# Moving the preparation of the next chunk, and one leaky relu, behind the copies of the finished output banks, in a spectral layer followed by a two-layer MLP

## The chip, the cores and the metric

One core of one Trainium2 chip. The metric is the device time of one execution in microseconds (us), the median of several runs. The engines named here are PE (TensorE; PEld is its weight load), DVE (VectorE), ACT (ScalarE), POOL (GpSimd) and SP (SyncE, which here only issues DMAs). All matmuls of the main loop run on fp32 data that is split into a high and a low fp32r part.

## The reference

Input x is (8, 3008, 256). First a spectral layer, then an MLP with leaky relu on all 24064 tokens:

```
X  = rfft(x, axis=1)
Yr = Xr @ w_r - Xi @ w_i + b_r ;  Yi = Xr @ w_i + Xi @ w_r + b_i
Y  = sign(Y) * max(|Y| - 0.01, 0)            # for Yr and Yi each
y  = irfft(Y, n=3008, axis=1).reshape(24064, 256)
h  = y @ w_in                                # 256 x 2048
out = max(0.01 * h, h) @ w_out               # 2048 x 256
```

## The kernel before

The length 3008 is 47 x 64, so the transform is done in two stages of small matmuls: `fwd` (the stage over 47), then `mid` (the stage over 64, the projection by w_r and w_i, the threshold, and the first inverse stage). They pass through DRAM as `u_dram` and `v_dram`. The second inverse stage, `inverse`, reads `v_dram` through the tile `vin` (one buffer, loaded by `v_load` on the SP queue) and writes tokens into the tiles `yc` (three buffers).

The MLP works on 32 chunks of 752 tokens, four to a batch; a chunk is two halves of 376. `moe()` is the main loop, and each chunk has two parts.

The **product part** loops over the eight q (256 of the 2048 hidden columns each). `moe_a` and `moe_b` compute the 2 x 2 block product by seven block products instead of eight, so the inputs are needed in seven combinations, the "forms" in the tile `yhl` (one buffer, high and low part). Each product is three matmuls of 376 columns into a bank `psh`. `moe_a` needs the forms 0, 3, 4 and 2 in this order, `moe_b` the forms 1, 6 and 5. ACT and DVE then add and apply the leaky relu (ACT `Prelu`). The first half's result `gf` is split at once into `gh` (ACT, L625) and `gl` (DVE, L626). The second half's result `gs` gets its leaky relu at L615 and waits in `s_t`; `late` splits it in the output part. Between `moe_a` and `moe_b` run the output products of the first half, two q behind.

The **output part** has 16 steps, each one call of `moe_o` (six matmuls into one of the two banks `pso`). The first four steps finish the two banks of the first half; ACT copies each to `ob` (L650) and SP stores it. The next steps need those two banks again, for the second half. `late` runs on the way: it splits `gs` of the next q into one of three pairs of `gg` buffers, as PE frees them. Also on the way, `forms(ci + 1)` prepares the next chunk: five pieces, each a few DVE subtractions and splits (L525 on ACT, L526 on DVE).

`fwd`, `mid` and the next chunk's `inverse` calls are streams that are mixed in between: the tokens generator takes one step per half q (16 per product part), `fwd` and `mid` advance with the position in the loop, such that the stream of a batch ends before the position `read[b]` at which `v_load` wants it.

What sets the order: the program is given in the order of these generators, and a planner issues each engine's instructions by that order as priority and by when its own timeline says that they are ready. `issue_after(x)` puts instructions behind x on x's engine; `in_order` keeps the MLP's matmuls in program order on PE. An instruction of a stream may be moved far ahead of its place. On the chip every engine then runs its list in order.

Of the kernel before, what the change touches and what calls it, by code (L numbers as in the profile page):

```python
# [12 lines left out]
AF = mybir.ActivationFunctionType  # L13
# [10 lines left out]
SLOPE = 0.01  # L24
# [6 lines left out]
def spectral_mlp_kernel(  # L31
# [17 lines left out]
    NB = x.shape[0]  # L49
# [5 lines left out]
    NQ = NF // 2  # L55
    HT, HP = N1 * N2 // 8, 192
    CT, HH = 2 * HT, HT // 2
# [8 lines left out]
    sync, act, dve, pool = nc.sync, nc.scalar, nc.vector, nc.gpsimd  # L66

    def bank(tag, bufs):
        return ps.tile([P, 512], F32, name=tag, tag=tag, bufs=bufs)
# [30 lines left out]
    def turned_halves(t):  # L100
        return t[:, :, :HH].rearrange("p a b -> p b a")

    def halves(t):
        return t.rearrange("p (a b) -> p a b", a=2)
# [47 lines left out]
        dve.tensor_mul(q, q, wl.bitcast(F32))  # L152


    made, converted, parted, early_parts = [], [], [], []


    NIN = DF // 4
# [310 lines left out]
    nch = p0[-1] // CT  # L469
    y_t, v_t, f_t, h_t, g_t, o_t, s_t = {}, {}, {}, {}, {}, {}, {}  # L470

    def v_load(pi):
        if pi == 1:
            vin = early[:PA, :4 * D].rearrange("p (c i d) -> p c i d", c=2, i=2)
        else:
            vin = sb.tile([PA, 2, 2, D], F32, name="vin", tag="vin", bufs=1)
        (b, s, _), n = pairs[pi][0], len(pairs[pi])
        vv = v_dram[b].rearrange("c k (g s) d -> c (k g) s d", g=NG)
        for c in range(2):
            ld = sync.dma_start(vin[:, c, :n, :], vv[c, :, s:s + n, :])  # L480
            if pi < 2:
                reads.append(ld)
        v_t[pi] = vin

    def inverse(pi, eh):


        n0, m = pairs[pi][0][2], sum(n for _, _, n in pairs[pi])
        ne, n = m * NK1, m * N1
        vin = v_t[pi]  # L490
        py = bank("psf", 2)
        s = slice(eh * P, (eh + 1) * P)
        for c in range(2):
            for i in range(len(pairs[pi])):
                o = c * ne + i * n0 * NK1
                nc.tensor.matmul(py[:, o:o + P], vin[:, c, i, s], consts["ga"][:, c, :], start=True, stop=True)  # L496
        odd = sb.tile([P, 2 * NG * NK1], F32, name="odd", tag="odd", bufs=1)[:, :ne]
        y = sb.tile([P, 2 * NG * N1], F32, name="y", tag="y")
        act.copy(odd, py[:, ne:2 * ne])
        dve.tensor_add(y[:, :ne], py[:, :ne], odd)  # L500
        ev, ov = (t.rearrange("p (m k) -> p m k", k=NK1)[:, :, 1:] for t in (py[:, :ne], odd))
        dve.tensor_sub(y[:, ne:n].rearrange("p (m k) -> p m k", m=m), ev, ov)
        lo = p0[pi]
        while lo < p0[pi + 1]:
            k = lo // HT
            hi = min((k + 1) * HT, p0[pi + 1])
            if k not in f_t:
                f_t[k] = sb.tile([P, NH, HT], F32, name="yc", tag="yc", bufs=3)
            act.copy(f_t[k][:, eh, lo - k * HT:hi - k * HT], y[:, lo - p0[pi]:hi - p0[pi]])
            lo = hi  # L510
# [49 lines left out]
    def product(dst, ci, q, k, start=False):  # L560
        form(dst, ci, q, AK[k - 1], BK[k - 1], start)

    def plain(ci, q, half):

        g0 = sb.tile([P, 2, 2, HP], F32, name="gs" if half else "gf", tag="gs" if half else "gf", bufs=NQ if half else 1)
        g = g0[:, :, :, :HH]
        for i, ((a, b), (a1, b1)) in enumerate((((0, 0), (1, 1)), ((3, 0), (2, 4)))):
            c = bank("psh", 4)
            form(c, ci, q, a, 2 * half + b, True)
            form(c, ci, q, a1, b1 + half if i else 2 * half + b1)  # L570
            act.activation(g[:, i], halves(c[:, :HT]), AF.Prelu, alpha=SLOPE)
        if half:
            s_t[ci, q] = g0
        else:
            parts(ci, q, 0, g0)
            early_parts[:] = parted
# [19 lines left out]
    def moe_b(ci, q):  # L596

        if ci == 0:
            return plain(ci, q, 1)
        c11, c21, c12, u, g1 = h_t.pop((ci, q))  # L600
        product(c11, ci, q, 2)
        product(c21, ci, q, 4)
        product(c12, ci, q, 3)
        g0 = sb.tile([P, 2, 2, HP], F32, name="gf", tag="gf", bufs=1)
        g = g0[:, :, :, :HH]
        act.activation(g[:, 0], halves(c11[:, :HT]), AF.Prelu, alpha=SLOPE)  # L606
        dve.tensor_add(g[:, 1], halves(c21[:, :HT]), halves(u))  # L607
        act.activation(g[:, 1], g[:, 1], AF.Prelu, alpha=SLOPE)  # L608
        g = g1[:, :, :, :HH]
        dve.tensor_add(g[:, 0], halves(c12[:, :HT]), halves(u))  # L610
        parts(ci, q, 0, g0)
        early_parts[:] = parted
        g = wide(g)
        with tc.issue_after(parted[0].ins):
            act.activation(g, g, AF.Prelu, alpha=SLOPE)  # L615
        s_t[ci, q] = g1

    def wide(t):
        return t.rearrange("p i a b -> p (i a) b")

    def parts(ci, q, half, g):
        gh, gl = g_t[ci, q, half] = tuple(
            sb.tile([P, 2, 2, HP], F32R, name=n_, tag="gg", bufs=6) for n_ in ("gh", "gl"))
        g, h, l = (wide(t)[:, :, :HH] for t in (g, gh, gl))
        cp = act.copy(h, g)  # L625
        parted[:] = [cp, dve.tensor_sub(l, g, h.bitcast(F32))]  # L626
# [5 lines left out]
    def moe_o(ci, q, h, eh):  # L632
        gh, gl = g_t[ci, q, h]
        wh, wl = consts["wout"]
        if q == 0:
            o_t[ci, h, eh] = bank("pso", 2)
        po = o_t[ci, h, eh][:, :HT]
        pv = po.rearrange("p (b a) -> p b a", a=2)
        s = slice(eh * P, (eh + 1) * P)
        for j, (a, r) in enumerate(((wh, gh), (wl, gh), (wh, gl))):  # L640
            for i in range(2):
                f = 2 * q + i
                mlp[:] = [nc.tensor.matmul(  # L643
                    pv, a[:, f, s], turned_halves(r[:, i]), start=(f == 0 and j == 0),
                    stop=(f == NF - 1 and j == 2),
                )]
        if q == NQ - 1:
            ob = sb.tile([P, HT], F32, name="ob", tag="y")
            with tc.high_priority(200):
                act.copy(ob, po)  # L650
            lo = ci * CT + h * HT
            sync.dma_start(out[s, lo:lo + HT], ob)

    due = [[p for p in range(len(pairs)) if p0[p] // CT == ci] for ci in range(nch)]
    UNITS = 45 * NQ
    read = [max(0, b * nch // NB - 1) + 51 / UNITS for b in range(NB)]

    def tokens(ci):

        for _ in range(3):  # L660
            yield
        for p in due[ci]:
            v_load(p)
            yield
            yield
            for eh in range(NH):
                inverse(p, eh)
                yield
                yield

    def moe():

        behind = []

        def next_o(eh, least=2):
            if len(behind) >= least:
                in_order(moe_o, *behind[0], eh)
                if eh:
                    behind.pop(0)

        for ci in range(nch):
            nxt = tokens(ci + 1) if ci + 1 < nch else iter(())
            units = 0
            for q in range(NQ):
                in_order(moe_a, ci, q)
                next_o(0)
                next(nxt, None)
                units += 18
                yield ci + units / UNITS
                in_order(moe_b, ci, q)  # L690
                next_o(1)
                behind.append((ci, q, 0))
                next(nxt, None)
                units += 15
                yield ci + units / UNITS
            for _ in nxt:
                pass
            nxt = forms(ci + 1) if ci + 1 < nch else iter(())
            behind += [(ci, q, 1) for q in range(NQ)]
            late(ci, 0)  # L700
            for q in range(0, NQ, 2):
                for k, eh in ((0, 0), (1, 0), (0, 1), (1, 1)) if q < 4 else ((0, 0), (0, 1), (1, 0), (1, 1)):
                    in_order(moe_o, *behind[q + k], eh)
                    if eh:
                        late(ci, q + k + 1)
                    with tc.issue_after(early_parts[0].ins), tc.issue_after(early_parts[1].ins):
                        next(nxt, None)
                    units += 6
                    yield ci + units / UNITS
            del behind[:NQ]  # L710
        while behind:
            for eh in range(NH):
                next_o(eh, 1)
# [215 lines left out]
```

## Time and profile before

| what | value |
|---|---|
| median of 3 runs | 2504.17 us (2503.83 to 2505.91) |
| the profiled execution | 2500.98 us |
| its span from first to last instruction | 2499.2 us |
| PE busy | 2419.7 us (97%) |
| DVE busy | 1848.5 us (74%) |
| ACT busy | 1652.7 us (66%) |
| POOL busy | 251.3 us (10%) |

The busy time of PE is a union of overlapping matmuls whose ends are modelled; what tells of lost time is when a matmul starts later than the one before it allows. The granted TensorE clock is full (1.00) from 130 us on. From chunk 8 on, at 746 us, the pattern of four chunks repeats batch after batch; the last batch has no more stream beside it from chunk 27 on.

### The profile page before, as it was taken

To read this page: it belongs to the slowest core of one execution; us is meant where nothing else is said; L and a number is where in the kernel's file an instruction comes from. 1 tells how busy PE (TensorE), PEld (TensorE's weight loads), DVE (VectorE), ACT (ScalarE), POOL (GpSimd) and SP (SyncE) were. 2 spreads that over 40 slices of the span, in tenths; PEclk is the share of its full clock that TensorE was granted. 3 is DMA by queue.
4 is the path that set the end of the run, shared out by engine and by line. 5 is a ranking of instruction groups with operands and counts; after the bars stand their busy time and mean duration, and the time that the engine had idled before them with its cause. 6 is when DMAs were issued, how large, how long until landed. Compare 5 with 4: busy or idle time off the path is not lost.

```text
span 2499.2 us, 41562 instructions
## 1 busy us (share of the span) xinstructions
PE 2419.7 (97%) x15412; PEld 2326.9 (93%) x15412; DVE 1848.5 (74%) x3197; ACT 1652.7 (66%) x3229; POOL 251.3 (10%) x192
## 2 busy tenths in 40 slices
PE   6899999999999999999999999999999999999999
PEld 4589999999999999999999999999999999999999
DVE  6777778777787777776787777777778777777675
ACT  4676766677667666676766676666766667756555
POOL 1200113000110001100021000210012000000000
PEclk8999999999999999999999999999999999999999
DMA  7632214221232112321132121331214211110000
GB/s 236 184 116 57 59 45 128 70 56 53 71 101 59 51 51 79 95 62 51 47 93 85 53 61 45 96 87 45 61 40 119 68 51 46 42 37 29 17 13 19
DMA packets 138479, 173.68 MB, mean 69 GB/s; under 512 B 15661, under 2 KB 100645, under 8 KB 138277
## 3 DMA queue, kind: packets, MB, share of 16 engines
q1 hardware_dynamic: 97688, 124.17, 16.7%
q10 hardware_dynamic: 40589, 46.87, 7.5%
q8 instruction: 121, 1.98, 0.3%
q14 instruction: 81, 0.66, 0.1%
HBM read 95.22 MB, written 75.76 MB: 68 GB/s over the span
## 4 chain that ended last, share of the span: by engine, by line
PE 79%; ACT 9%; DVE 5%; DMA 3%; issue 2%; SPq 0%; ACTq 0%; POOL 0%; DVEq 0%
PE pso L643 33%; PE psh L98 29%; PE psf L82 11%; PE psf L496 3%; PE psf L365 2%; ACT gh L625 1%; ACT zf L417 1%; DMA vin<-v_dram 1%; DVE t L407 1%; ACT gs L615 1%; ACT zf L413 1%; PE psh L82 1%; DMA v_dram<-v 1%; ACT gf L608 1%; DVE gf L607 1%
## 5 line engine op out<-in xcount | busy, mean ns | idle before, releaser
L98 PE MATMUL psh<-yhl,win_hi 128*128 128x376 f32 x3600 | 894.8, 331 | 16.1 <-DVE gs L592 14.3
L98 PEld LDWEIGHTS psh<-yhl,win_hi 128*128 128x128 f32 x3600 | 607.4, 190 | 45.6 <-DVE gs L592 22.8
L98 PE MATMUL psh<-yhl,win_lo 128*128 128x376 f32 x1800 | 580.5, 322 | 0.0
L643 PE MATMUL pso<-gh,wout_hi 128*128 128x376 f32 x2048 | 496.6, 324 | 9.4 <-ACT ob L650 9.2
L643 PE MATMUL pso<-gl,wout_hi 128*128 128x376 f32 x2048 | 497.7, 325 | 0.8 <-DVE gl L626 0.6
L643 PE MATMUL pso<-gh,wout_lo 128*128 128x376 f32 x2048 | 493.3, 322 | 0.0
L643 PEld LDWEIGHTS pso<-gh,wout_hi 128*128 128x128 f32 x2048 | 354.3, 189 | 13.0 <-ACT ob L650 12.3
L643 PEld LDWEIGHTS pso<-gl,wout_hi 128*128 128x128 f32 x2048 | 354.1, 189 | 7.8 <-DVE gl L626 6.4
L643 PEld LDWEIGHTS pso<-gh,wout_lo 128*128 128x128 f32 x2048 | 356.6, 189 | 0.0
L98 PEld LDWEIGHTS psh<-yhl,win_lo 128*128 128x128 f32 x1800 | 340.0, 189 | 0.3 <-issue 0.2
L626 DVE TENSOR_TENSOR gl<-gf,gh 128x752 fp32r<-128x752 f32 x256 | 244.6, 956 | 115.9 <-ACT gh L625 114.5
L399 POOL TENSOR_TENSOR kb<-bias,kc 128x512 f32<-128x512 f32 x96 | 138.9, 1447 | 1592.3 <-ACT kc L397 1516.0
L626 DVE TENSOR_TENSOR gl<-gs,gh 128x752 fp32r<-128x752 f32 x256 | 238.8, 939 | 53.6 <-ACT gh L625 52.5
L606 ACT ACTIVATE gf<-psh 128x376 f32<-128x376 f32 x248 | 120.9, 487 | 224.6 <-PE psh L98 217.2
L625 ACT CAST gh<-gs 128x752 fp32r<-128x752 f32 x256 | 209.4, 820 | 76.5 <-PE pso L643 65.3
L608 ACT ACTIVATE gf<-gf 128x376 f32<-128x376 f32 x248 | 128.5, 518 | 162.8 <-DVE gf L607 153.5
L591 DVE TENSOR_TENSOR p<-psh,p 128x376 f32<-128x376 f32 x248 | 136.0, 548 | 121.0 <-ACT p L590 106.1
L625 ACT CAST gh<-gf 128x752 fp32r<-128x752 f32 x256 | 210.2, 821 | 9.3 <-issue 1.1
L615 ACT ACTIVATE gs<-gs 128x752 f32<-128x752 f32 x248 | 205.6, 829 | 1.9 <-DVE gs L610 0.9
L607 DVE TENSOR_TENSOR gf<-psh,p 128x376 f32<-128x376 f32 x248 | 135.1, 545 | 68.6 <-PE psh L98 67.9
L593 DVE TENSOR_TENSOR gs<-psh,gs 128x376 f32<-128x376 f32 x248 | 135.6, 547 | 21.7 <-PE psh L98 3.3
L592 DVE TENSOR_TENSOR gs<-psh,p 128x376 f32<-128x376 f32 x248 | 135.6, 547 | 18.9 <-PE psh L98 0.6
(139 smaller groups left out, 3520.0 us busy)
## 6 DMA issues: line engine op xcount, KB each, us to landing
u<-u_dram SPq DMA_DIRECT2D x192, 128.0 KB, 2.7
v_dram<-v ACTq DMA_DIRECT2D x192, 128.0 KB, 2.4
out_dram<-ob SPq DMA_DIRECT2D x128, 188.0 KB, 1.9
vin<-v_dram SPq DMA_DIRECT2D x94, 240.0 KB, 3.5
xin<-x_dram SPq DMA_DIRECT2D x90, 240.0 KB, 3.0
u_dram<-xin ACTq DMA_DIRECT2D x72, 240.0 KB, 2.4
fb<-fb_dram SPq DMA_DIRECT2D x96, 96.0 KB, 2.0
u_dram<-xin SPq DMA_DIRECT2D x24, 240.0 KB, 3.9
```

Source lines behind the costliest of these rows:

```text
L82: last = nc.tensor.matmul(dst, a, b, start=(i == 0), stop=(i == len(terms) - 1))
L98: mlp[:] = [nc.tensor.matmul(dst, a, b, start=start and i == 0, stop=i == 2, skip_group_check=True)]
L399: pool.tensor_add(kb, bias, kc.unsqueeze(1).broadcast_to([P, 2, D]))
L591: dve.tensor_add(u, c22[:, :HT], u)
L592: dve.tensor_add(g[:, 1], halves(c21[:, :HT]), halves(u))
L593: dve.tensor_add(g[:, 1], halves(c12[:, :HT]), g[:, 1])
L607: dve.tensor_add(g[:, 1], halves(c21[:, :HT]), halves(u))
L608: act.activation(g[:, 1], g[:, 1], AF.Prelu, alpha=SLOPE)
L615: act.activation(g, g, AF.Prelu, alpha=SLOPE)
L625: cp = act.copy(h, g)
L626: parted[:] = [cp, dve.tensor_sub(l, g, h.bitcast(F32))]
L643: mlp[:] = [nc.tensor.matmul(pv, a[:, f, s], turned_halves(r[:, i]), start=(f == 0 and j == 0), stop=(f == NF - 1 and j == 2),)]
```

## The change

It does five things. `forms` is stepped from q = 2 of the output part on instead of q = 0, and its instructions are put behind the ACT copy of the last finished output bank (`copied[0]`) in place of the last `gh` cast (`early_parts[0]`); on DVE they stay behind the last `gl` (`early_parts[1]`). The leaky relu of `gs` for q = 7 is no longer issued in `moe_b` but with the first step of `forms`, also behind the copy. The tokens generator waits two steps instead of three before its first `v_load`, three instead of two between `v_load` and `inverse`, and has one step instead of two per `inverse`: the two `v_load` of a chunk go from steps 4 and 10 to 3 and 8, the four `inverse` from 6, 8, 12 and 14 to 6, 7, 11 and 12. `read` goes from 51 to 33 units of 360 in a chunk. `kept` is the former leaky relu as a function.

```diff
@@ moe_b
         early_parts[:] = parted
-        g = wide(g)
-        with tc.issue_after(parted[0].ins):
-            act.activation(g, g, AF.Prelu, alpha=SLOPE)
         s_t[ci, q] = g1
+        if q < NQ - 1:
+            with tc.issue_after(parted[0].ins):
+                kept(g1)
+
+    def kept(g1):
+        g = wide(g1)[:, :, :HH]
+        act.activation(g, g, AF.Prelu, alpha=SLOPE)
@@ moe_o
             with tc.high_priority(200):
-                act.copy(ob, po)
+                copied[:] = [act.copy(ob, po)]
@@
-    read = [max(0, b * nch // NB - 1) + 51 / UNITS for b in range(NB)]
+    read = [max(0, b * nch // NB - 1) + 33 / UNITS for b in range(NB)]
@@ tokens
-        for _ in range(3):
+        for _ in range(2):
             yield
         for p in due[ci]:
             v_load(p)
-            yield
-            yield
+            for _ in range(3):
+                yield
             for eh in range(NH):
                 inverse(p, eh)
-                yield
                 yield
@@ moe
-                    with tc.issue_after(early_parts[0].ins), tc.issue_after(early_parts[1].ins):
-                        next(nxt, None)
+                    if q:
+                        with tc.issue_after(copied[0].ins), tc.issue_after(early_parts[1].ins):
+                            if ci and (q, k, eh) == (2, 0, 0):
+                                kept(s_t[ci, NQ - 1])
+                            next(nxt, None)
```

## Rows read from the trace of the kernel before

**Rows 1.** Waits of PE, 140 us to the end: us, times, longest.
```profile
PE psh L98 <- DVE gs L592: 14.3, 22, 1.3
PE pso L643 <- ACT ob L650: 9.2, 5, 1.8
PE psf L82 <- ACT eh L380: 8.6, 15, 1.0
PE psf L496 <- DMA vin<-v_dram: 6.6, 7, 1.4
PE pso L643 <- DVE gl L626: 0.6, 3, 0.2
```
**Rows 2.** Timeline of ACT, output part of chunk 12: start us, us, instruction.
```profile
1109.83 0.81 ACT L525 CAST yhl<-yc 128x752 fp32r<-128x752 f32 x1
1110.55 0.82 ACT L615 ACTIVATE gs<-gs 128x752 f32<-128x752 f32 x1
1111.28 0.39 ACT L413 COPY zf<-t 64x256 f32<-64x256 f32 x1
...
1114.77 0.51 ACT L525 CAST yhl<-yt 128x376 fp32r<-128x376 f32 x1
1115.18 0.47 ACT L650 COPY ob<-pso 128x376 f32<-128x376 f32 x1
```
**Rows 3.** Timeline of PE, same stretch; in brackets idle time and its releaser.
```profile
1113.05 0.48 PE L643 MATMUL pso<-gh,wout_lo 128*128 128x376 f32 x2
1113.37 0.48 PE L643 MATMUL pso<-gl,wout_hi 128*128 128x376 f32 x2
1115.69 0.59 PE L643 MATMUL pso<-gh,wout_hi 128*128 128x376 f32 x2 [1.84 <-ACT ob L650]
```
**Rows 4.** Timeline of the SP queue, output part of chunk 14.
```profile
1269.16 0.32 SPq L480 DMA_DIRECT2D vin<-v_dram  x1
...
1270.02 0.37 SPq L480 DMA_DIRECT2D vin<-v_dram  x1
```
**Rows 5.** Timeline of PE, output part of chunk 14.
```profile
1273.74 0.71 PE L496 MATMUL psf<-ga,vin 120*128 120x128 f32 x4 [0.70 <-DMA vin<-v_dram]
```
**Rows 6.** Timeline of DVE, output part of chunk 28.
```profile
2303.83 0.54 DVE L526 TENSOR_TENSOR yhl<-yt,yhl 128x376 fp32r<-128x376 f32 x1
2304.29 0.93 DVE L626 TENSOR_TENSOR gl<-gs,gh 128x752 fp32r<-128x752 f32 x1
...
2309.93 0.54 DVE L526 TENSOR_TENSOR yhl<-yc,yhl 128x376 fp32r<-128x376 f32 x1
```
**Rows 7.** Timeline of PE, chunk 28: second `gl` used; first matmul of chunk 29.
```profile
2305.28 0.59 PE L643 MATMUL pso<-gl,wout_hi 128*128 128x376 f32 x2
...
2315.25 0.48 PE L98 MATMUL psh<-yhl,win_hi 128*128 128x376 f32 x2
```
**Rows 8.** Timeline of ACT, chunk 28: first form split, second copy.
```profile
2300.82 0.80 ACT L525 CAST yhl<-yc 128x752 fp32r<-128x752 f32 x1
...
2304.47 0.47 ACT L650 COPY ob<-pso 128x376 f32<-128x376 f32 x1
```
**Rows 9.** Waits of PE, chunks 2 to 5 (286 to 602 us).
```profile
PE psf L82 <- ACT eh L380: 2.1, 4, 1.0
PE psh L98 <- ACT p L590: 0.8, 1, 0.8
```
**Rows 10.** Waits of PE, chunks 10 to 13 (905 to 1208 us).
```profile
PE psf L82 <- ACT eh L380: 1.3, 2, 0.6
```
**Rows 11.** Windows, output parts of chunks 13 and 14: PE, PEld, DVE, ACT, POOL busy.
```profile
1187.17:1208.24 21.07, 21.07 (x145) 20.99 (x143) 19.44 (x30) 16.93 (x31) 1.76 (x1) 1.00 0.18 50
1262.02:1282.38 20.36, 19.66 (x121) 19.03 (x121) 19.01 (x27) 14.09 (x24) 3.17 (x3) 1.00 0.33 93
```
**Rows 12.** Timeline of POOL, output part of chunk 13.
```profile
1193.00 1.76 POOL L399 TENSOR_TENSOR kb<-bias,kc 128x512 f32<-128x512 f32 x1 [12.24 <-ACT kc L397]
```
**Rows 13.** Timeline of DVE, output part of chunk 13.
```profile
1193.52 1.65 DVE L526 TENSOR_TENSOR yhl<-yt,yhl 128x376 fp32r<-128x376 f32 x1
```

More of the change, by code (lines that the diff above doesn't have):

```diff
@@ L152, in float64_parts @@
         dve.tensor_mul(q, q, wl.bitcast(F32))
-    made, converted, parted, early_parts = [], [], [], []
+    made, converted, parted, early_parts, copied = [], [], [], [], []
     NIN = DF // 4
```

## Prediction

> **What bounds the kernel now.** I read the busy shares first, then the waits of PE, then the timelines of the longest of them. The busy shares in the table put PE far ahead of DVE and ACT, so the time is PE's list of matmuls plus the moments in which PE stands. The waits of PE behind the start-up [rows 1] show how little there is to win: five kinds, 39.3 us together (14.3 + 9.2 + 8.6 + 6.6 + 0.6). Two of them belong to the change by name. The wait for `ob` L650 occurs only 5 times, and each is almost as long as the longest, 1.8 us; it is in every fourth chunk from chunk 8 to 24. The wait for `vin` occurs 7 times. The other large ones, `gs` L592 and `eh` L380, lie in the product parts, which the change touches only through the streams beside them.
>
> The timelines of chunk 12 show why `ob` is late. ACT runs without a gap there, and in front of the first copy at 1115.18 stand the first split of a form at 1109.83, the leaky relu at 1110.55 and the second split of a form at 1114.77 [rows 2]. PE starts pairs of matmuls 0.32 us apart (1113.05, 1113.37), so the next pair was due at 1113.69; it starts at 1115.69, 2.0 us late, released by the copy [rows 3]. The recorded idle time, 1.84, is a little less, since the end of a matmul is modelled.
>
> **The change part by part.** No instruction is added or removed; the matmuls and DMAs stay the same in number and size. Everything is order.
>
> *The three ACT instructions that leave the place in front of the copy.* From start to start they hold ACT for 0.72 us (1109.83 to 1110.55), 0.73 us (to 1111.28) and 0.41 us (1114.77 to 1115.18), 1.86 us in all [rows 2]. The copy then starts at 1113.32. It ends 0.47 us later and PE followed its start by 0.51 us, so PE goes on at 1113.83: 0.14 us late where it was 2.0. That is 1.86 us in each of 5 chunks, 9.3 us. The second copy of the same chunk loses one more form split ahead of it, and PE's short hold there is covered as well by what the first copy gains; I count 0.2 us a chunk for it, an estimate. Together 10.3 us, rounded to 10. Bounds: at most the whole wait, 5 x (2.0 + 0.3) = 11.5; at worst nothing, if the planner puts other stream work in the place that comes free; a loss only where the copies themselves got later, which nothing does, as all three instructions are pinned behind them.
>
> *The forms, later.* They cost nothing as long as they end before the next chunk reads them. In chunk 28, where no stream helps to hide them, their first split starts on ACT at 2300.82 and the second copy, behind which they now go, ends at 2304.94 [rows 8]: a shift of 4.1 us. Their last DVE split ends at 2310.47 [rows 6], and chunk 29 starts at 2315.25 [rows 7], so 4.8 us of cover become 0.7. The last piece is form 6, which is wanted only after five products of three matmuls and one output step of six, 21 x 0.16 = 3.4 us later (0.16 is half of the 0.32 above); the cover is then some 4 us. Value: 0. If the shift were 2 us longer than this in all 31 chunks and the cover gone, each us beyond it would cost 31 us; that is the rival on the slower side, below. What is late next is not the forms but `gl`.
>
> *The `gl` just in time.* In chunk 28 the `gl` of the second q starts at 2304.29 right behind a form's split of 0.54 us [rows 6]; it ends at 2305.22, and PE picks it up at 2305.28 [rows 7]. I count such a tight place in every second chunk and 0.2 us for each, an estimate from these rows; only 0.6 us in all are long enough for a row among the waits [rows 1]. With the form gone from in front of it, 16 x 0.2 = 3 us could go. Against it the forms now stand among the third to fifth `gl`. I take 2 us off; bounds 3 off and 3 more.
>
> *The leaky relu of q = 7.* It takes part in the 1.86 us. Behind the copy it is wanted by the eighth `gh` alone, many steps later: 0.
>
> *`v_load` and `inverse` sooner.* In chunk 14 the two halves of `vin` are issued at 1269.16 and 1270.02 [rows 4], and PE stands 0.70 us for the second at 1273.74 [rows 5]. The chain before it (the last copy of `v` on ACT, its store) is in the same stretch in which three ACT instructions leave, and the stream of a batch must now end 18 units of 360 sooner. Both move the load forward; but the planner moves `inverse` forward by the same rule, and the wait is there because its own timeline holds the chain for shorter than it is. So half: 6.6 us [rows 1] give 3. Bounds: all 6.6, or a gain of nothing and the same again lost, +6.6. On the SP queue the second load of a chunk now stands two steps sooner behind the first pair's matmuls and holds what is behind it (`u`, `xin`, `ob` stores); PE has no wait for `u` or `xin` in the main loop [rows 1], so this costs 0.
>
> *The product parts in a new alignment.* The streams run 18 units earlier against the chunks, and two `inverse` come one step apart, where they were two. Which products meet which stream copies changes, and with it the waits for L592 and L380, 22.9 us [rows 1]. No row shows the new alignment. The trace has two: chunks 2 to 5 have 2.9 us of `eh` and `p` waits [rows 9], the steady chunks 10 to 13 have 1.3 [rows 10]. Between them lies 1.6 us a batch, 10 us over six batches; that is the upper bound, and 10 off is the lower, about half of what is there. The one other alignment that the trace shows is the dearer one, so I take a third of the upper bound, +3.
>
> Sum, against the profiled execution: 2500.98 - 10 - 2 - 3 + 3 = 2489.0. That execution lies 3.2 us below the median of the runs; on the median's level it is 2504.2 - 12 = 2492.
>
> **The rivals.**
>
> *The wait changes its name.* ACT's place in front of the copy is filled by other stream copies, or PE, 2 us earlier at the copy, runs into `gl` a step later. For it: `gl` is already just in time in many chunks. Against it: after 1115 in chunk 12 the work that has left has to be done anyway, and PE waits for none of it today. The gain is then 0 to 4 us: 2502.
>
> *DVE falls behind; slower.* In the output parts of chunks 13 and 14 DVE is busy for 19.44 of 21.07 us and 19.01 of 20.36 [rows 11]; 1.6 and 1.35 us are free. Today the first two pieces of the forms (three DVE instructions of 0.54 us and one as long as a `gl`, 0.93 [rows 6], 2.55 us) fill the time before the copies. If nothing else is ready there, that time is lost and the work comes back later: 0.9 + 1.2 us a batch reach the next product part, where PE's largest wait, L592, is one for DVE. Over six batches 12.7 us. One more price belongs to it: in chunk 13 a form's split took 1.65 us in place of 0.54 [rows 6, 13] while POOL's addition ran from 1193.00 to 1194.76 [rows 12]; a split that meets POOL in its new place adds 1.1 us, 6.7 us over six batches. With the 10 us from `ob` kept this gives 2504.2 - 10 + 19 = 2513. It decides from about 1.6 us of new DVE idle time ahead of the first form. For it: the windows. Against it: the cover of 4 us, and stream work on DVE that the planner can put forward. The Trainium skill speaks on this side (SBUF — State Buffer, Who interferes with whom): a DVE instruction that reads two operands from SBUF contends with a POOL instruction that reads SBUF. The row of the 1.65 us agrees; by the rule every form's split and subtraction is of this kind, so a longer hold than in the row is possible wherever POOL's additions run.
>
> *More than forecast.* The new alignment also clears half of the product parts' waits: 22.9 / 2 = 11 us more, 2478.
>
> *It does not do what it says.* `copied[0]` is an ACT instruction, so the DVE halves are not held by it; the first subtraction may run early. This alters nothing for the copy and is no case of its own.
>
> **How the numbers follow.** Forecast 0.53 (2492; its own range 2485 to 2499), a changed name 0.20 (2502), DVE behind 0.17 (2513), more 0.10 (2478). About 0.2% or 5 us is what a measurement of this kernel tells from no change. Faster by more than that: 0.53 + 0.10 = 0.63; within: 0.20; slower: 0.17. The range goes from 2483, where half of the best case is left out, to 2507, where most of DVE's is.
>
> **What would show it.** Right: the wait of PE for `ob` falls from 9.2 us to under 2, the copy in the output part of chunk 12 has no L525 or L615 among the ACT instructions before it, and the first products of a chunk have no wait for `yhl`. The `vin` wait should halve. Wrong: a wait of PE for `yhl` L525 or L526, a longer total for L592, or DVE idle in front of the first form. If L592 and L380 together grow by more than 10 us, the gain is gone, and the step that failed is the alignment.

## The result and the profile after

The changed kernel takes 2465.47 us (median of 4 runs, 2463.41 to 2466.68); the kernel before, in the same job, 2504.0. The ratio is 0.9847, with a 95% interval of 0.9834 to 0.9859: 38 us faster where 12 were forecast, and below the whole range of 2483 to 2507. The direction held, the size did not.

In the page of the changed kernel, the busy shares:

```profile
PE 2404.8 (98%) x15412; PEld 2327.8 (94%) x15412; DVE 1876.0 (76%) x3197; ACT 1662.1 (67%) x3229; POOL 277.3 (11%) x192
```

PE has the same 15412 matmuls and is busy for 14.9 us less than the 2419.7 before. So part of what PE lost was booked as busy time: a matmul that starts after a wait is longer in the record (0.59 us beside 0.48 in [rows 3]). The waits of PE of the changed kernel, 140 to 2440 us (us, times, longest), answer to [rows 1]; behind 2440 none is recorded:

```profile
PE psf L82 <- ACT eh L380: 5.9, 11, 0.6
PE psh L98 <- ACT p L590: 2.9, 5, 0.6
PE psh L98 <- DVE gs L593: 2.9, 7, 0.9
PE psh L98 <- DVE gs L592: 2.5, 8, 0.5
PE pso L647 <- DVE gl L630: 1.6, 2, 1.3
PE psf L496 <- DMA vin<-v_dram: 1.4, 1, 1.4
PE psf L82 <- DVE xz L270: 0.7, 2, 0.5
PE pso L647 <- ACT ob L654: 0.5, 1, 0.5
PE psf L365 <- DMA u<-u_dram: 0.2, 1, 0.2
```

`ob` fell from 9.2 to 0.5, `vin` from 6.6 to 1.4, L592 from 14.3 to 2.5. All recorded waits fell by 21.8 us, to 18.6 from 40.4 (the whole list before: beside the five kinds of [rows 1], which the prediction took for all, it has `p` L590 with 0.8 and L593 with 0.3); with the 14.9 that is 36.7, about the 35.4 by which the span fell (2499.2 to 2463.8).

To see in which part the time went I also counted PE's *late time*: for each matmul behind the start-up, the time from the last matmul's start to its own, less what that shape takes when nothing holds it (0.159 us at 376 columns), wherever the rest is 0.09 us or more. It takes in what the record books as busy. The product part of a chunk goes here from its first product (L98) to its last; the rest is its output part.

| late time, us | product parts | output parts |
|---|---|---|
| before | 50.7 | 26.5 |
| after | 31.8 | 11.1 |
| difference | -18.9 | -15.4 |

Together -34.3, again about the span's difference. Over half of the gain is in the product parts, where the forecast had 3 us of loss. Timeline of ACT of the changed kernel, the end of chunk 12; it answers to [rows 2]:

```profile
1099.05 0.47 ACT L654 COPY ob<-pso 128x376 f32<-128x376 f32 x1 [0.38 <-PE pso L647]
1099.71 0.82 ACT L629 CAST gh<-gs 128x752 fp32r<-128x752 f32 x1 [0.19 <-issue]
1100.76 0.48 ACT L654 COPY ob<-pso 128x376 f32<-128x376 f32 x1 [0.23 <-PE pso L647]
1101.13 0.83 ACT L629 CAST gh<-gs 128x752 fp32r<-128x752 f32 x1
1101.86 0.82 ACT L620 ACTIVATE gs<-gs 128x752 f32<-128x752 f32 x1
1102.59 0.81 ACT L525 CAST yhl<-yc 128x752 fp32r<-128x752 f32 x1
```

Before, PE waited for ACT at the first copy; now ACT stands idle for 0.38 us until PE has filled the bank. The leaky relu (now L620) and the first form split come behind the second copy and one `gh` cast.

### The profile page after: what moved, and what is told of

Same layout as the page of the kernel before. It is cut to its first block, busy times and chain, and to the rows that moved or that the text cites. A ratio compares the mean times of both kernels' runs of the same rounds, so it can differ in the third digit from the quotient of the medians.

```text
span 2463.8 us, 41538 instructions
## 1 busy us (share of the span) xinstructions
PE 2404.8 (98%) x15412; PEld 2327.8 (94%) x15412; DVE 1876.0 (76%) x3197; ACT 1662.1 (67%) x3229; POOL 277.3 (11%) x192
## 4 chain that ended last, share of the span: by engine, by line
PE 86%; ACT 6%; DVE 3%; DMA 2%; issue 1%; SPq 0%; ACTq 0%; POOL 0%; DVEq 0%
PE pso L647 36%; PE psh L98 32%; PE psf L82 11%; PE psf L496 3%; PE psf L365 2%; ACT zf L417 1%; ACT gh L629 1%; ACT zf L413 1%; PE psh L82 1%; DMA xin<-x_dram 1%; DVE t L407 1%; ACT gf L608 0%; DVE gf L607 0%; ACT gs L620 0%; DMA fb<-fb_dram 0%
## 5 line engine op out<-in xcount | busy, mean ns | idle before, releaser
L98 PE MATMUL psh<-yhl,win_hi 128*128 128x376 f32 x3600 | 887.4, 329 | 8.4 <-ACT p L590 2.9
L98 PEld LDWEIGHTS psh<-yhl,win_hi 128*128 128x128 f32 x3600 | 611.0, 190 | 30.0 <-DVE gs L593 7.7
L98 PE MATMUL psh<-yhl,win_lo 128*128 128x376 f32 x1800 | 580.7, 323 | 0.0
L647 PE MATMUL pso<-gh,wout_hi 128*128 128x376 f32 x2048 | 497.4, 324 | 1.2 <-ACT ob L654 0.5
L647 PE MATMUL pso<-gl,wout_hi 128*128 128x376 f32 x2048 | 497.0, 324 | 1.6 <-DVE gl L630 1.6
L647 PE MATMUL pso<-gh,wout_lo 128*128 128x376 f32 x2048 | 493.4, 322 | 0.0
L647 PEld LDWEIGHTS pso<-gl,wout_hi 128*128 128x128 f32 x2048 | 354.1, 189 | 6.5 <-DVE gl L630 5.0
L647 PEld LDWEIGHTS pso<-gh,wout_hi 128*128 128x128 f32 x2048 | 354.1, 189 | 4.9 <-ACT ob L654 2.2
L647 PEld LDWEIGHTS pso<-gh,wout_lo 128*128 128x128 f32 x2048 | 356.5, 189 | 0.0
L98 PEld LDWEIGHTS psh<-yhl,win_lo 128*128 128x128 f32 x1800 | 340.0, 189 | 0.2 <-issue 0.2
L630 DVE TENSOR_TENSOR gl<-gf,gh 128x752 fp32r<-128x752 f32 x256 | 250.7, 979 | 109.9 <-ACT gh L629 107.8
L630 DVE TENSOR_TENSOR gl<-gs,gh 128x752 fp32r<-128x752 f32 x256 | 252.4, 994 | 30.9 <-ACT gh L629 29.9
L629 ACT CAST gh<-gs 128x752 fp32r<-128x752 f32 x256 | 208.5, 820 | 44.8 <-PE pso L647 34.2
L620 ACT ACTIVATE gs<-gs 128x752 f32<-128x752 f32 x248 | 205.5, 829 | 4.6 <-DVE gs L610 4.3
L591 DVE TENSOR_TENSOR p<-psh,p 128x376 f32<-128x376 f32 x248 | 135.6, 547 | 67.5 <-ACT p L590 49.0
L593 DVE TENSOR_TENSOR gs<-psh,gs 128x376 f32<-128x376 f32 x248 | 135.8, 548 | 21.5 <-PE psh L98 2.7
L592 DVE TENSOR_TENSOR gs<-psh,p 128x376 f32<-128x376 f32 x248 | 135.8, 548 | 19.9 <-PE psh L98 0.8
```

The lines of the kernel that those rows point to most:

```text
L98: mlp[:] = [nc.tensor.matmul(dst, a, b, start=start and i == 0, stop=i == 2, skip_group_check=True)]
L591: dve.tensor_add(u, c22[:, :HT], u)
L593: dve.tensor_add(g[:, 1], halves(c12[:, :HT]), g[:, 1])
L647: mlp[:] = [nc.tensor.matmul(pv, a[:, f, s], turned_halves(r[:, i]), start=(f == 0 and j == 0), stop=(f == NF - 1 and j == 2),)]
```

## The experiments

Each kernel is the one before or the one after with one part of the change done or undone. All edits come from four pieces: *forms* (the forms' steps pinned behind the copy, only from the second `q` on), *relu* (that of `q` = 7 behind the copy), *tokens* (the new steps between `v_load` and `inverse`) and *read* (51 to 33). The kernels ran in several jobs, each with the kernel before beside them on the same chip; it gave medians of 2501.1 to 2504.0 there, and ratios are against the one of the same job. Late times are those of the one profiled execution, which can lie off the median: it took 2501.07 for relu alone, 2479.49 for forms from `q` = 4 and 2518.57 for `eh` behind the adds.

| kernel | us | ratio (95%) | late: products | outputs |
|---|---|---|---|---|
| forms + relu | 2481.29 | 0.9916 (0.9901–0.9931) | 51.4 | 5.8 |
| tokens + read | 2491.53 | 0.9956 (0.9940–0.9973) | 24.1 | 41.4 |
| read alone, 33 | 2486.74 | 0.9938 (0.9923–0.9953) | 21.7 | 41.0 |
| forms alone | 2494.17 | 0.9968 (0.9955–0.9981) | 54.4 | 15.4 |
| relu alone | 2497.94 | 0.9982 (0.9973–0.9991) | 39.8 | 36.9 |
| read alone, 42 | 2494.82 | 0.9971 (0.9956–0.9983) | 35.5 | 34.3 |
| read alone, 18 | 2507.90 | 1.0023 (1.0014–1.0032) | 34.2 | 51.9 |
| read alone, 0 | 2492.33 | 0.9959 (0.9944–0.9974) | 33.3 | 34.9 |
| after, read 18 | 2462.17 | 0.9842 (0.9828–0.9857) | 24.2 | 16.3 |
| after, old tokens | **2446.56** | 0.9776 (0.9761–0.9791) | 14.7 | 9.8 |
| forms + relu, read 42 | 2470.48 | 0.9875 (0.9858–0.9892) | 26.8 | 17.5 |
| after, forms from `q` = 4 | 2477.09 | 0.9896 (0.9881–0.9911) | 45.4 | 10.2 |
| after, pin of before | 2489.92 | 0.9954 (0.9938–0.9971) | 24.0 | 42.3 |
| before, `eh` behind the adds | 2513.90 | 1.0037 (1.0024–1.0051) | 40.8 | 53.3 |

**The two halves of the change.** Forms + relu, with tokens and read as before:

```
# after.py with
-    read = [... + 33 / UNITS ...]      # and the old tokens()
+    read = [... + 51 / UNITS ...]
```

> The forms and the one leaky relu are moved as in the change; tokens and read stay as before. Theory A (the product parts gained because inverse and the streams meet other products): only the wait for the ob copy goes, some 10 us, so about 2494; the vin wait (6.6 us) and the gs L592 wait (14.3 us) stay within 3 us. Theory B (the work that left the front of the output parts let the planner order everything better): most of the 38.5 us, 2475 or less, and gs L592 under 7 us. Theory C (every new order scatters the product parts' waits by 10 us or more either way): the ob wait goes, but the total lies anywhere from 2480 to 2505 and the parts will not add up to the whole.

It took 2481.3: 20.7 us less, all in the output parts (26.5 to 5.8). Theory A had 2494, theory B 2475 or less; neither came. The total lies in the wide range of theory C. Its waits of PE, first lines (140 to 2440 us):

```profile
PE psh L98 <- DVE gs L592: 11.3, 19, 0.8
PE psf L82 <- ACT eh L380: 8.0, 12, 1.2
PE psh L98 <- DVE gs L593: 2.4, 11, 0.3
PE psf L496 <- DMA vin<-v_dram: 1.9, 3, 1.4
```

No `ob` row is left, and `vin` fell to 1.9 although neither `v_load` nor `read` was touched. The likely reason is ACT's chain in front of the load, which got free; no run shows it by itself. The product parts keep their waits.

The other half, tokens + read, and read by itself:

```
# before.py with
-    read = [... + 51 / UNITS ...]
+    read = [... + 33 / UNITS ...]      # the first of the two also has the new tokens()
```

> The tokens' steps and read are changed as in the change; forms and the leaky relu stay before the copies. Theory A: the ob wait stays near 9 us, vin falls to under 2 us and gs L592 to under 5 us: some 25 us, about 2479. Theory B: 5 us at most, 2499 or more, gs L592 stays over 10 us. Theory C: a total that does not complement the first run's to 38.5 us; the sum of both gains misses it by more than 8 us.

> Only read goes from 51 to 33 units; v_load and inverse keep their steps, so inverse's input is ready one part sooner than it is asked for. Theory A with the weight on the streams' place: most of what the second run gains, about 2482. Theory A with the weight on the steps of v_load and inverse: 0 to 5 us, about 2500, but the vin wait falls to under 2 us since the data is there sooner. Theory C: anything within 12 us of before.

They took 2491.5 and 2486.7. Read alone takes 29 us of late time out of the product parts and gives 14.5 back in the output parts. Its waits of PE (140 to 2440 us):

```profile
PE pso L643 <- ACT ob L650: 12.8, 7, 1.9
PE pso L643 <- DVE gl L626: 9.2, 13, 1.3
PE psh L98 <- DVE gs L593: 3.4, 8, 1.0
PE psh L98 <- DVE gs L592: 2.4, 9, 0.4
```

L592 is almost gone, and the gain is hidden behind longer waits for `ob` and `gl`. The new tokens cost 4.8 us here. The two halves, 20.7 and 10.4, make 31.1 of the 38.5 us of the change; theory C asked for a miss of more than 8, and it is some 7.

**Forms and relu apart.**

```
# before.py, forms alone:
+ if q:
+     with tc.issue_after(copied[0].ins), tc.issue_after(early_parts[1].ins):
+         next(nxt, None)
# before.py, relu alone: the old forms' steps, and behind them
+ if ci and (q, k, eh) == (2, 0, 0):
+     with tc.issue_after(copied[0].ins):
+         kept(s_t[ci, NQ - 1])
```

> The forms alone are moved behind the copies; the leaky relu of q = 7 stays in moe_b, in front of the first copy, where it holds ACT for 0.73 us; tokens and read stay. By the sum of the prediction the ob wait keeps 0.73 us + 0.1 in each of 5 chunks, so it falls from 9.2 to about 4 us and the total lies 4 us above the first run's. Theory C: the difference to the first run is more than 8 us either way, from the product parts.

> Before with only the leaky relu of q = 7 moved behind the copies. By ACT's queue in front of the first copy: 0.73 us in 5 chunks, so the ob wait falls from 9.2 to about 5.5 us and the total by 4 us, to 2497. If the relu was worth what the first and the fourth experiment differ by (12.9 us), 2488, and the waits for eh and vin fall too. Scatter: 2485 to 2505 with the ob wait still near 5.5.

Measured: 7.8 and 4.3 us less than before; together they give 20.7, so the sum is not the whole. Forms alone lies 12.9 us above forms + relu, where 4 were expected; relu alone has the total that was expected (2497). The waits of PE say where the rest is, first for forms alone, then for relu alone (both 140 to 2440 us):

```profile
PE psf L82 <- ACT eh L380: 10.4, 17, 1.2
PE pso L643 <- ACT ob L650: 3.8, 6, 0.8
```

```profile
PE psf L365 <- DMA u<-u_dram: 8.3, 5, 3.3
...
PE pso L647 <- DVE gl L630: 3.5, 9, 0.6
PE pso L647 <- ACT ob L654: 3.3, 5, 0.7
```

Forms take 5.4 and relu 5.9 off the 9.2 us of `ob`: both hold the copy, as the prediction had it. By their time on ACT [rows 2] their shares were 5.7 and 3.7. But relu alone brings waits for `u` (8.3) and `gl` (3.5), where the kernel before has 0 and 0.6 and forms + relu has no such row. In its trace the output parts are 10.4 us later than before (36.9 against 26.5) and the product parts 10.9 us sooner. That execution, the slowest of the ten, took as long as the profiled one of before (2500.98), so the trace does not show where the 4.3 us of the median come from. Why relu alone reorders the streams so is not settled.

**Is it the pin?** The changed kernel with the same steps, pinned behind the instruction of before:

```
- with tc.issue_after(copied[0].ins), tc.issue_after(early_parts[1].ins):
+ with tc.issue_after(early_parts[0].ins), tc.issue_after(early_parts[1].ins):
```

> The changed kernel with the forms and the one leaky relu in the steps from q = 2 on, but not put behind the copies: behind the last early gh cast, as before. If the place in program order is enough, 2465 within 6 and no ob wait over 2 us. If the pin on the copy does it, some of the seven pieces of ACT work slip in front of the copy again: an ob wait of 4 us or more and 2472 or above.

2489.9, as tokens + read (2491.5) within their spreads. First line of its waits of PE (140 to 2440 us):

```profile
PE pso L647 <- ACT ob L654: 11.1, 6, 1.8
```

Later steps of the loop alone are worth nothing; what moves the work is the one `issue_after` on the copy.

**How much room the forms have.** The changed kernel with forms two `q` later, pinned behind the last `gh` and `gl` of `late` instead of the copy (the leaky relu stays behind the copy):

```
+ if q > 2:
+     with tc.issue_after(parted[0].ins), tc.issue_after(parted[1].ins):
+         next(nxt, None)
```

> The changed kernel with the forms' five pieces put later still, from q = 4 on, each behind the last gh and gl of late. The cover is then used up: the forms' last splits end 2.2 to 4.8 us before the next chunk in the changed kernel, and the shift is some 4 us, with form 3 wanted 0.5 us into the chunk. If the cover is what keeps the move free, PE waits for yhl (L525, L526) by 0.5 to 2 us in most of 31 chunks: 2480 to 2525. If it isn't, no wait for yhl and 2465 within 8.

2477.1, 11.6 us more than the change, and not the 2480 or more expected. No long wait for a form came (one of 0.3 us). PE waits at L592 instead, 10.2 us in all; 10 of these 17 waits, 7.1 us, are in the first `q` of a chunk. Its timeline, all engines, at the start of chunk 28 (the last split of a form, the last output step and the wait):

```profile
2229.35 0.54 DVE L526 TENSOR_TENSOR yhl<-yc,yhl 128x376 fp32r<-128x376 f32 x1
...
2229.64 0.48 PE L647 MATMUL pso<-gh,wout_hi 128*128 128x376 f32 x2
...
2231.51 0.55 DVE L591 TENSOR_TENSOR p<-psh,p 128x376 f32<-128x376 f32 x1 [1.61 <-PE psh L98]
2232.09 0.55 DVE L592 TENSOR_TENSOR gs<-psh,p 128x376 f32<-128x376 f32 x1
2232.69 0.59 PE L98 MATMUL psh<-yhl,win_hi 128*128 128x376 f32 x2 [0.82 <-DVE gs L592]
```

DVE was idle for 1.61 us before L591, so it was not busy with forms. The output step of the old chunk (L647 at 2229.64) now stands behind eight of the twelve matmuls of `moe_a`, where in the changed kernel it follows all twelve; the products behind it come too close for the additions. So a lost cover shows as a worse list for PE, not as a wait by the form's name. It is not the whole price. Of the 13.6 us by which the late time of the product parts rises in this trace (31.8 to 45.4), 6.2 lie at one place in chunk 3: PE waits 2.98 us for `zh` there (L424, at 375.95), and the granted clock is 0.50 for 6.8 us.

**Which alignment?** Three other values of `read` in the kernel before, to see whether sooner is better or whether one phase of the streams against the chunks is:

```
- + 51 / UNITS
+ + 42 / UNITS   (and 18, and 0)
```

> Before with read at 42 units of 360, all else as before. In program order the stage that starts a chain of ACT and DVE work (the 64-point stage, eh) comes 7 times in 12 right behind moe_a with read at 51, 4 times with 33, counted from the code. Theory phase (the product parts lose where that stage falls between moe_a and moe_b, so only the place against the parts counts): 42 also gives 4 of 12, so gs L592 and eh L380 together fall below 8 us as with 33 (3.2 us), and the total is near 2487. Theory sooner is better (the waits shrink with the streams' lead): about half way, 2494, with gs L592 near 8 us. Theory scatter: no relation, 2480 to 2505.

> Before with read at 18 units. Theory phase: the stage comes 7 times in 12 behind moe_a again, as with 51, so gs L592 and eh L380 together come back to over 16 us (22.9 before) and the total is near 2500. Theory sooner is better: below read at 33, 2484 or less, gs L592 under 2.4 us. Theory scatter: anything from 2480 to 2505.

> Before with read at 0 units. Theory phase: 4 times in 12 behind moe_a, as with 33, so gs L592 and eh L380 together under 8 us; the total near 2487. Theory sooner is better: 2480 or less. Theory scatter: anything from 2480 to 2505.

2494.8, 2507.9 and 2492.3. Neither theory holds: 18 is sooner than 33 and is slower than 51; and 18, bad for the product parts by the theory of phases, has 34.2 us there, like 42 and 0, which were to be good. What is left is scatter, and even its bound of 2505 is passed by 18. What 42, 33, 18 and 0 share is that 51 is the worst of the five for the products (50.7 against 21.7 to 35.5) and the best for the outputs (26.5 against 34.3 to 51.9).

The change with 18, and with the old tokens, and forms + relu at 42:

```
# after.py: 33 -> 18;   after.py with the old tokens();   the latter with 33 -> 42
```

> The changed kernel with read at 18 units in place of 33. Theory phase: the product parts' waits (gs L592 and L593, p L590, eh L380: 14.2 us in the changed kernel) go up by 10 us or more, to the level of the first experiment (22.5 us), and the total to about 2478. Theory sooner is better: the same as the changed kernel or below, 2465 or less. Theory scatter: anything from 2460 to 2485.

> The changed kernel with the steps of v_load and inverse of before (4, 6, 8, 10, 12, 14); forms, leaky relu and read at 33 as changed. If the move out of the front of the output parts is worth the same at every alignment of the streams, this lies as far under read at 33 alone (2486.7) as the first experiment lies under before: 2466, give or take 5, and the output parts wait for ob and gl under 4 us where the read experiment had 22. If the steps of inverse carry part of the gain, 2472 or more. Scatter of the product parts alone: 2455 to 2480.

> The forms and the leaky relu behind the copies, tokens as before, read at 42. The same with forms in front is 2494.8. If the move is worth 20 us or more at every alignment, 2475 or less, with the ob wait under 2 us (11.0 with forms in front) and the gl wait under 2 (4.2). If its worth at 33 was luck of that alignment, 2480 or more.

2462.2, 2446.6 and 2470.5: the first as "sooner is better" had it, which 18 in the kernel before had refuted; the second below every expectation; the third as expected, but for a `gl` wait of 3.6. So forms + relu behind the copies gain 20.7 us at 51, 24.3 at 42, 40.2 at 33 with the old tokens, and 26.1 at 33 with the new ones (rows with the same read and tokens, forms in front and behind; the last three compare two jobs, whose medians of before lie up to 2.1 us apart). Old tokens with the rest of the change is the best version: 56 us or 2.2% below the kernel before of its job, 19 below the change. Its waits of PE (140 to 2440 us), the first lines:

```profile
PE psf L496 <- DMA vin<-v_dram: 1.6, 1, 1.6
PE pso L647 <- ACT ob L654: 1.6, 7, 0.5
```

**What carries the waits of the products?** In the trace of before, the timelines of ACT, of DVE and of PE at a wait for L592:

```profile
1093.39 0.40 ACT L413 COPY zf<-t 64x256 f32<-64x256 f32 x1
...
1095.26 0.83 ACT L615 ACTIVATE gs<-gs 128x752 f32<-128x752 f32 x1
1095.99 0.46 ACT L590 COPY p<-psh 128x376 f32<-128x376 f32 x1
```

```profile
1096.48 0.55 DVE L591 TENSOR_TENSOR p<-psh,p 128x376 f32<-128x376 f32 x1 [2.03 <-ACT p L590]
1096.95 0.40 DVE L500 TENSOR_TENSOR y<-psf,odd 128x240 f32<-128x240 f32 x1
1097.26 0.39 DVE L502 TENSOR_TENSOR y<-psf,odd 128x230 f32<-128x230 f32 x1
1097.57 0.54 DVE L592 TENSOR_TENSOR gs<-psh,p 128x376 f32<-128x376 f32 x1
```

```profile
1098.16 0.59 PE L98 MATMUL psh<-yhl,win_hi 128*128 128x376 f32 x2 [0.76 <-DVE gs L592]
```

The wait has two holders. First ACT: DVE stands idle for 2.03 us before L591, until ACT has copied the first product to `p` (L590). ACT copies late, since four instructions of `mid` (`zf`: L413 and L417, twice) stand in front of it from 1093.39 to 1095.26, and the leaky relu behind them. Then DVE: two additions of `inverse` stand between L591 and L592 and hold L592 for 0.62 us (0.31 + 0.31 from start to start). PE waits for 0.76.

Of the 22 waits for L592 in this trace, 18 (11.4 of 14.3 us) lie behind such an idle time of DVE that ends with `p`; in 10 of them (7.5 us) the two additions of `inverse` come on top, in the other 8 nothing stands between L591 and L592. Counted by ACT, all four `zf` instructions stand between the first product and its `p` in 19 of 248 `q`, and these have 12.3 of the 15.4 us of recorded waits for L590, L592 and L593. With read alone at 33 it is 7 `q` and 4.3 of 5.8 us, in the changed kernel 18 and 7.2 of 8.3, in the best one 2 and none of 2.0. The number of such `q` is not all: it hardly differs between before and after, while the waits do. Nor are they the only holder: in the changed kernel with read 18 it is 0.7 of 8.5 us. No run moved these four by themselves, so this is read from traces and not tested.

What I tested was DVE alone. Counted over the trace, 101 of 248 `q` have another instruction inside the chain of three additions (in 14 only a `gl` of the MLP itself), and these have 15.5 us of waits of the products; the 147 others have 0.6. In the changed kernel it is 7.9 to 0.5, in the best one 1.6 to 0.4; with read 18 in the changed kernel it is not so (4.4 to 4.2). The two of `inverse` are the most frequent, 59 times before and 76 after; those that get rarer as the waits do are the two of `eh` (L378, L379): 42 times in the chains of before, 18 after, 4 in the best. So I put these behind the chain, in the kernel before:

```
- dve.tensor_add(xi, ...); dve.tensor_sub(el[...], ...)
+ with tc.issue_after(added[0].ins):          # added: the last addition of the chain, L593
+     dve.tensor_add(xi, ...); dve.tensor_sub(el[...], ...)
```

> Before (read at 51, forms in front of the copies) with one order added: the two DVE instructions that start a stage's eh chain (xi L378 and eh L379, 0.42 and 0.68 us) are put behind the last add of the last traced moe_a (L593). In DVE's list 42 of them stand inside a moe_a chain of adds in before, 8 here. Theory inside (moe_b's second product waits for the second add, and what holds it is stream work inside the chain): gs L592 falls from 14.3 us to 6 or less and the total by 8 us or more, to 2494 or below. Theory alignment without a carrier (the product parts' waits move with the matmuls' places, whatever stands in DVE's list): L592 stays over 10 us. The ob wait stays at 7 us or more either way, as the front of the output part is as in before.

It took 2513.9 (10 runs), about 10 us more than before. The kernel has one line more ahead of these, so `gl` is L627 and the second and third additions are L593 and L594; its waits of PE (140 to 2440 us):

```profile
PE pso L644 <- DVE gl L627: 18.9, 18, 2.0
PE psh L98 <- DVE gs L593: 9.1, 23, 1.1
PE psh L98 <- DVE gs L594: 6.2, 11, 0.6
```

The wait for the second addition fell from 14.3 to 9.1, not to the 6 expected, and the third rose from 0.3 to 6.2; late time of the products fell by 10, and that of the outputs doubled. The expectation had a fault that the trace of before shows: all 42 instructions stand behind the second addition there, between L592 and L593, so none of them could hold L592. The theory is not borne out by this run. Nor is all of the loss one of order: in this trace the granted clock falls to 0.50 seven times in the output parts, which takes 11.8 of their 53.3 us of late time (the last section shows one). The mean granted clock of its ten runs is 0.9915, of the thirteen of before beside them 0.9937; by the seven stretches and the 0.006 that they make in the trace, that is two to three stretches a run, some 4 of the 10 us, an estimate. How the planner's order comes to put the streams' instructions in front of `p` or into the chain in one alignment and not in another stays open.

## Why the prediction was wrong

**The step that failed** is "The product parts in a new alignment", the term of +3. Measured, it is -29.0 us of late time for read alone, -18.9 in the whole change; in the recorded waits L592 and L380 together went from 22.9 to 8.4. The fault was in how it was bounded. "Half of what is there" was no bound, only a number; the waits of 22.9 us were all in reach, and the late time of the product parts, 50.7, is more than twice as much. With the measured term the sum is 2492 - 3 - 19 = 2470, close to what came. Instead I read two stretches of one trace as two alignments, put the untried one near the dearer of them, and counted with a sign that no row supported. The five values of `read` show that 51 was the dearest for the products and that any other value tried takes 15 to 29 us from them: the most frequent waits of the trace belong in good part to that one value. The rival "more than forecast" (2478, a chance of 0.10) named the right place with half its size. By name L592 is a wait for DVE, and the prediction took it for one; in 18 of 22 cases DVE itself stood for ACT's `p`.

That the rest of the sum comes out is partly luck. The terms of -10, -2 and -3 make -15, and the output parts measure -15.4; but this is -20.7 for forms + relu, of which `read` takes part back (+14.5 when it is alone).

**The `ob` wait**, -10: right. 9.2 to no row with forms + relu, by two halves of 5.4 and 5.9, and to 0.5 in the whole change; the pin is the cause, shown by its removal. With forms + relu the output parts won 20.7, twice the term: 9.2 are the row of `ob` and 4.7 that of `vin`; most of the rest is in no row of waits.

**`vin` sooner**, -3: 6.6 to 1.4 is -5.2, within the bounds. Each of the two reasons given does it without the other: forms + relu leave 1.9 at the old `read`, read alone leaves 1.2. But the rewritten steps of `tokens`, which belong to the same edit, cost 4.8 us without and 18.9 with forms moved, and the prediction counted that edit as a gain.

**`gl` just in time**, -2: not seen. The wait for `gl` is 1.6 after against 0.6, a miss of a size that decides nothing. Yet with forms in front and `read` at 33 it is 9.2, so the term was worth more in the alignment that the change brings than in the one that I read it from. With forms in front, `ob` and `gl` make 22.0 us of waits at 33 and 9.8 at 51. That is 12 of the 20 us by which forms behind the copies gain more there (40.2 against 20.7): the parts of the change are not a sum.

**The forms, later**, 0: right. No wait for a form is recorded. The timeline of the changed kernel in chunk 28, all engines: second copy, first and last split of a form, start of chunk 29; it answers to [rows 6 to 8]:

```profile
2269.57 0.47 ACT L654 COPY ob<-pso 128x376 f32<-128x376 f32 x1
...
2270.67 0.81 ACT L525 CAST yhl<-yc 128x752 fp32r<-128x752 f32 x1
...
2277.62 0.54 DVE L526 TENSOR_TENSOR yhl<-yc,yhl 128x376 fp32r<-128x376 f32 x1
...
2280.43 0.48 PE L98 MATMUL psh<-yhl,win_hi 128*128 128x376 f32 x2
```

The cover is 2.3 us (2278.16 to 2280.43); before it was 4.8, forecast 0.7. It was not far from its end: the kernel with forms two `q` later is 11.6 slower, in part through the one place in chunk 3.

**DVE falls behind** did not come. L592 fell, and DVE's idle time before the first split of a form in chunk 28 is 0.87 us, under the 1.6 at which the rival was to decide. One price on that side was right by itself: more DVE instructions meet POOL. Those over 0.2 us longer than usual while a POOL operation runs rose from 44 to 68, and what they take beyond their usual time from 31.0 to 59.9 us; DVE's busy time rose by about as much, 1848.5 to 1876.0 in the pages. But PE lost little by it: of its late time in the output parts 0.6 of 26.5 us before, and 1.5 of 11.1 after, comes within 5 us of the start of such an instruction. One of the 68, timeline of POOL and DVE of the changed kernel:

```profile
1098.75 1.89 POOL L399 TENSOR_TENSOR kb<-bias,kc 128x512 f32<-128x512 f32 x1 [11.75 <-ACT kc L397]
...
1099.40 1.65 DVE L541 TENSOR_TENSOR yc<-yc 128x376 f32<-128x376 f32 x1
```

L541 takes 1.65 us in place of 0.54 (it takes 0.54 in chunk 28 at 2267.81), and PE does not wait for it. The rule of the Trainium skill that the prediction cited (SBUF — State Buffer, Who interferes with whom) agrees with the row as to the hold; what the hold costs, the order decides.

## What to carry to other kernels

When an order by a planner decides, ask of each wait whether it belongs to the work or to the place that the streams happen to have against it: move the streams by one constant and look, since here one value of `read` was worth 15 us alone and 35 us together with another edit. Bound such a term by all the waits in reach, on both sides, and not by a share of them. When a wait is for DVE by name, look at what DVE stood for before. Pin work that nobody awaits behind the copy that somebody awaits, and test the parts of a change together: its best version here was the change without one of its edits.

## What the runs showed of the hardware

A recorded idle time of PE understates what a wait costs. The 1.84 us of [rows 3] were 2.0 us of start to start, and the matmul behind it took 0.59 in place of 0.48 and so held the next; over the trace 14.9 us of the gain were booked as busy time of an unchanged number of matmuls.

A POOL operation can make DVE late enough for PE to stand. In the kernel with `eh` behind the adds 16.3 of the 53.3 us of late time in the output parts come within 5 us of the start of a lengthened DVE instruction (2.2 of them are the lower clock, below). Its timeline of DVE and POOL, then of PE, at one of the longest waits:

```profile
1585.15 1.35 POOL L260 TENSOR_TENSOR xs<-xin,xin 120x512 f32<-120x512 f32 x1 [4.04 <-PE pso L644]
1585.28 1.50 DVE L409 TENSOR_SCALAR c<-t 128x512 f32<-128x512 f32 x1
1586.58 1.34 POOL L261 TENSOR_TENSOR xin<-xin,xin 120x512 f32<-120x512 f32 x1
1586.70 1.62 DVE L527 TENSOR_TENSOR yhl<-yt,yhl 128x376 fp32r<-128x376 f32 x1
```

```profile
1589.69 0.59 PE L644 MATMUL pso<-gl,wout_hi 128*128 128x376 f32 x2 [1.99 <-DVE gl L627]
```

Elsewhere the two DVE instructions take 0.42 and 0.54 us; each takes 1.08 us more beside a POOL operation of 1.35 and 1.34. Their 2.2 us of excess stand ahead of the `gl` for which PE then waits for 1.99. The first of them reads one operand only, which I had not counted among the instructions that POOL can hold. That the collisions cause the waits elsewhere is an association in time: taking POOL's additions away also changes the planner's order, so it was not tried.

The granted clock of TensorE can fall behind a wait. In the same kernel it goes from 1.00 to 0.50 (2.4 to 1.2 GHz) seven times between 976 and 1901 us, for 3.4 us each, and each time 0.2 to 1.1 us after the start of a matmul that had waited 1.66 to 2.00 us for `gl`. The stretch behind the wait above, as a window (length; PE, PEld, DVE, ACT and POOL busy; granted clock, DMA):

```profile
1590.80:1594.10 3.30, 3.30 (x12) 3.30 (x11) 2.24 (x4) 2.64 (x5) 0.00 (x0) 0.50 0.00 0
```

Pairs of matmuls start 0.63 us apart there instead of 0.32. PE is busy all the time, so no wait is recorded, and each stretch takes 1.7 us. In the kernel before, none of the five waits of 1.84 us for `ob` has such a stretch behind it; the length of the wait alone does not tell when it comes.
